# One product a head for the memory update, on the four column strips of TensorE

## The chip, the cores and the metric

The kernel runs on one core of one Trainium2 chip. The metric is the device time of one execution in microseconds (us). All five engines of the core are used: TensorE (PE, with PEld for its weight loads), VectorE (DVE), ScalarE (ACT), GpSimdE (POOL) and SyncE (SP), which only issues transfers.

## The reference

A layer normalisation feeds two branches whose results are added to the input: attention in four blocks of 512 tokens with a memory that is carried from block to block (16 heads of 28), and a gated feed-forward part.

```python
for s in range(N):                       # N = 4 blocks of L = 512 tokens
    qs, ks, vs = q[:, :, s], k[:, :, s], v[:, :, s]
    p = softmax(qs @ ks.T * scale + mask)
    a_dot = p @ vs
    pq = phi(qs)                         # phi(t) = t + 1 where t > 0, else exp(t)
    num = einsum("bhld,bhde->bhle", pq, M)
    den = einsum("bhld,bhd->bhl", pq, z)[..., None] + 1e-6
    outs.append(g * (num / den) + (1.0 - g) * a_dot)
    pk = phi(ks)
    M = M + einsum("bhld,bhle->bhde", pk, vs)
    z = z + einsum("bhld->bhd", pk)
return x + concat(outs) @ wo + (sigmoid(xn @ w_gate) * (xn @ w_up)) @ w_down
```

M is 28 x 28 a head, z a vector of 28. The kernel keeps z as one more column of M, by a column of ones beside the values.

## The kernel before

**Stages.** In a front part, the four blocks of tokens are normalised, turned, and projected to values (L361, pv), keys and queries (L381, pp); products in a split form of float32 take 11 passes each. The feed-forward part (L255, L181), the attention's scores (L639) and its sums over values (L725) follow, woven into each other by a hand-made plan, and the output projection (L824) ends the kernel. All of the change lies in the front part.

**A block of the front part** runs over `values` for four groups of 128 tokens, then `keys_queries` for seven groups of 128 columns (k = 0 to 6; four hold keys, which share the fourth with queries). Behind them, by `if`s on k, stand:

- `key_rows(k - 2)`: four transposes (pk, L401) bring a group of phi(keys) to token rows, and ScalarE copies them to kn (L403);
- `update(b, i)` (L405 to L416): the memory of four heads at a time, i = 0 to 3. Four products over 128 tokens each make a 112 x 128 tile (pmm) of phi(keys) of 4 heads by values of 4 heads. Only its diagonal blocks (28 x 32) are wanted, so VectorE multiplies it by `heads`, a mask of ones and zeros that GpSimdE builds (L522 to L527), and adds it to the memory of before. Updates 0 and 1 stand at k = 4 and 5, updates 2 and 3 at k = 6. Blocks 0, 1 and 2 update; block 3 does not;
- `turn`: transposes of the next block's tokens (pt, L103).

**The memory** is `mst[n][i]`, two sets of four tiles of 112 rows (28 a head) by 128 columns (32 a head).

**Reading the memory.** `keys_queries` stores phi(queries) to DRAM (fd, L394); `phi_queries` (L418) reads 112 rows of four heads back as phi; `recall` (L423) multiplies the memory by phi (n, L427), and VectorE divides the result. The recalls of blocks 1 and 2 are run between the values of the next block, those of block 3 between its projections.

**Order.** In the front part TensorE, ScalarE and VectorE run in the order in which the code is written (`tc.manual_schedule(engines=FRONT)`); GpSimdE and SyncE have an order that the framework sets. Accumulators have eight banks: pk, pmm and n share the tags "m" and "pd", of one bank each.

Of the kernel before, what the change touches and what calls it, by code (L numbers as in the profile page):

```python
# [9 lines left out]
F32 = mybir.dt.float32  # L10
F32R = mybir.dt.float32r
AF = mybir.ActivationFunctionType
ALU = mybir.AluOpType
# [3 lines left out]
P = 128  # L17
D = 448
H = 16
DH = 28  # L20
S = 2048
NB = 4
L = 512
NT = 4
F = 1792
NF = F // P
HG = 4
NG = H // HG
GW = HG * DH
# [40 lines left out]
def kernel(  # L70
# [10 lines left out]
    nc = tc.nc  # L81
    V, A, G, T = nc.vector, nc.scalar, nc.gpsimd, nc.tensor

    keep = ctx.enter_context(tc.tile_pool(name="keep", bufs=1))
    dram = ctx.enter_context(tc.tile_pool(name="dram", bufs=1, space=DRAM))
# [37 lines left out]
    def bank(name, tag):  # L123
        return ps.tile([P, L], F32, name=name, tag=tag, bufs=banks[tag])
# [5 lines left out]
    def pad(pool, nbytes):  # L130
        pool.tile([P, nbytes // 4], F32, name="pad", tag="pad", bufs=1)
# [3 lines left out]
    def weigh(pool, num, g, add):  # L135

        r = pool.tile([P, 16], F32, name="rc", bufs=2)
        n3 = num.rearrange("p (m c) -> p m c", c=32)
        if add:
            V.tensor_scalar_add(r, n3[:, :, DH], add)  # L140
            V.reciprocal(r, r)
        else:
            V.reciprocal(r, n3[:, :, DH])
        V.scalar_tensor_tensor(n3[:, :, :DH], n3[:, :, :DH], g, r.unsqueeze(2).to_broadcast([P, 16, DH]),
                               op0=ALU.mult, op1=ALU.mult)

    qd = [dram.tile([2 * D, 2, L], F32, name=f"qd{b}") for b in range(NB)]
    fd = [dram.tile([D, L], F32, name=f"fd{b}") for b in range(NB)]
    vd = [dram.tile([P, NT, H * 32], F32, name=f"vd{b}") for b in range(NB)]
    od = [dram.tile([H * 32, L], F32, name=f"od{b}") for b in range(NB)]  # L150

# [2 lines left out]
    def eight_k(dtype, name):  # L154
        return mid.tile([P, 8, 256], dtype, name=name, tag="8k")
# [144 lines left out]


    with tc.tile_pool(name="front", bufs=2) as sb, tc.manual_schedule(engines=FRONT):
        heads = sb.tile([P, P], F32, name="heads", bufs=1)
        pad(sb, 192)
        stage = eight_k(F32, "stage").rearrange("p (c a) n -> p c (a n)", c=4)
        vst = eight_k(F32, "vst").rearrange("p (t a) (h c) -> p t (a h) c", t=NT, c=32)
        wv = [late_pair("wv") for _ in range(4)]
        wv = [wv[c // 2][:, c % 2, :] for c in range(8)]
        wqk = [sb.tile([P, 8, P], F32R, name=f"wqk{c}", bufs=1) for c in range(7)]
        mst = [[sb.tile([GW, P], F32, name=f"mst{n}_{i}", bufs=1) for i in range(NG)] for n in range(2)]  # L310
        one = sb.tile([P, 1], F32, name="one", bufs=1)
        kn = eight_k(F32, "kn").rearrange("p (t a) n -> p t (a n)", t=NT)

# [55 lines left out]
        def values(b, t):  # L369
            pv = bank("pv", "p")  # L370
            value_terms(b, t, pv, EARLY[1] if b == 0 else TERMS)
            store_values(b, t, pv)
# [29 lines left out]
            n = min(P, D - c * P)  # L402
            A.activation(kn[:, :, c * P:c * P + n], pk.rearrange("p (t n) -> p t n", t=NT)[:, :, :n], AF.Copy)  # L403

        def update(b, i):  # L405

            pmm = bank("pmm", ("pd", "m")[i % 2])
            for t in range(NT):
                T.matmul(pmm[:GW, :P], kn[:, t, i * GW:(i + 1) * GW], vst[:, t, HG * i:HG * (i + 1), :],  # L409
                         start=t == 0, stop=t == NT - 1)  # L410
            if b == 0:
                V.tensor_mul(mst[1][i], pmm[:GW, :P], heads[:GW])
            else:
                dm = sb.tile([GW, P], F32, name="dm")
                V.tensor_mul(dm, pmm[:GW, :P], heads[:GW])
                V.tensor_add(mst[(b + 1) % 2][i], mst[b % 2][i], dm)  # L416

        def phi_queries(b, i):  # L418
            phi = sb.tile([GW, L], F32, name="phi", tag="e", bufs=5)
            nc.sync.dma_start(phi, fd[b][i * GW:(i + 1) * GW])  # L420
            return phi

        def recall(b, i, phi):  # L423
            ts = sb.tile([P, L], F32, name="ts", bufs=1)
            tb = sb.tile([P, L], F32, name="tb", bufs=2)
            n2 = bank("n2", ("m", "pd")[i % 2])
            T.matmul(n2, mst[b % 2][i], phi, start=True, stop=True)  # L427
            V.transpose(ts, n2)
            weigh(sb, ts, gate[:, i:i + 1], MEM_EPS)
            V.transpose(tb, ts)  # L430
            nc.gpsimd.dma_start(od[b][P * i:P * (i + 1)], tb)
# [28 lines left out]
        def split_qk(c):  # L460
            r = raw_qk[c].rearrange("p (c n) -> p c n", c=4)
            A.activation(wqk[c][:, 0:4, :], r, AF.Copy)
            G.tensor_sub(wqk[c][:, 4:8, :], r, wqk[c][:, 0:4, :].bitcast(F32))
# [18 lines left out]
        p3, xn, st, y = {}, {}, {}, {}  # L482
# [20 lines left out]
        for t in range(2):  # L503
# [15 lines left out]
        turn_low(3)  # L519
        split_qk(1)  # L520
        split_qk(2)
        G.memset(heads, 1.0)  # L522
        h3 = heads.rearrange("p (j c) -> p j c", c=32)
        G.affine_select(h3, h3, pattern=[[-DH, HG], [0, 32]], base=0, channel_multiplier=1,
                        compare_op=ALU.is_ge, fill=0.0)
        G.affine_select(h3, h3, pattern=[[DH, HG], [0, 32]], base=DH - 1, channel_multiplier=-1,
                        compare_op=ALU.is_ge, fill=0.0)  # L527

        ffn = gated()
        for b in range(NB):  # L530
            last = b == NB - 1
            phi, xn = {}, {}
            if b > 1:
                phi = {i: phi_queries(b - 1, i) for i in range(NG)}
            st = None
            for t in range(3 if b == 0 else 0, NT):
                values(b, t)
                if b > 1 and t > 0:
                    recall(b - 1, t - 1, phi[t - 1])
                if b == 0:  # L540
                    split_qk(t)
                if last:
                    continue
                if t == (3 if b == 0 else 0):
                    mv, vh = statistics(b + 1, 0, NT)
                if t == (3 if b == 0 else 0):
                    st = mv, vh, root(vh)
                if t == (3 if b == 0 else 2):
                    A.activation(one, ident[:, 0:1], AF.Exp)
            if st and b > 0:  # L550
                st = rstd(*st)
                for n in range(2):
                    xn[n] = normalise(b + 1, n, *st[n])
            e = {}
            for k, c in enumerate((3, 4, 5, 6, 0, 1, 2) if last else range(7)):
                e[c] = keys_queries(b, c)
                if b == 0 and c + 4 < 7:
                    split_qk(c + 4)
                if k == 0:
                    if b > 1:  # L560
                        recall(b - 1, NG - 1, phi[NG - 1])
                    if b == 0:
                        st = rstd(*st)
                    if b == 0:
                        A.activation(gate, gate, AF.Exp, scale=-1.0)
                        V.tensor_scalar_add(gate, gate, 1.0)
                        V.reciprocal(gate, gate)
                        V.tensor_scalar(gate_n, gate, -1.0, 1.0, op0=ALU.mult, op1=ALU.add)
                if (b, k) in ((0, 3), (1, 0)):
                    with tc.issue_after(stored[b, c]):  # L570
                        nc.sync.dma_start(acc[b + 2], x_block(b + 2))
                if (b, k) in ((2, 1), (3, 0)):
                    with tc.issue_after(stored[b, c]):
                        next(ffn)
                if last:
                    if k > 0:
                        next(ffn)
                    if 2 <= k < 6:
                        phi[k - 2] = phi_queries(b, k - 2)
                    if k > 4:  # L580
                        begin[k - 5]()
                        recall(b, k - 5, phi[k - 5])
                    continue
                if 2 <= k < 6:
                    key_rows(k - 2, e[k - 2])
                if 4 <= k:
                    update(b, k - 4)
                if k == 6:
                    update(b, 3)
                n = k - 1 if b == 0 else k + 1  # L590
                if 2 <= n < 6:
                    turn(b + 1, n - 2, xn[n - 2])
                if 0 <= n < 4 and n not in xn:
                    xn[n] = normalise(b + 1, n, *st[n])
                if b == 2 and k == 6:
                    next(ffn)
            if last:
                for i in range(2):
                    for _ in range(FILLS[i]):
                        next(ffn)  # L600
                    if i == 0:
                        begin[2]()
                    recall(b, i + 2, phi[i + 2])
# [3 lines left out]
    sb = ctx.enter_context(tc.tile_pool(name="att", bufs=1, reuse_waits="tile"))  # L607
# [234 lines left out]
    with tc.manual_schedule(engines=MANUAL):  # L842
        next(steps)
        k = sum(FILLS) + 6
# [46 lines left out]
```

## Time and profile before

| | |
|---|---|
| time, three runs | 685.53, 685.65, 686.12 us; median 685.65 |
| profiled execution, first to last instruction | 684.2 us (its device time is not shown apart from this span) |
| TensorE busy | 678.0 us, 99% |
| VectorE, ScalarE, GpSimdE busy | 570.1, 338.5, 141.6 us |
| front part | about 0 to 156 us |
| passes of the update (L409) | 96, from 34.4 to 115.0 us |
| VectorE's part of the update (L412, L415, L416) | 20 operations, 5.6 us |

A row of the profile's timeline has the start, the time from the first start to the last end, the engine, the line, the operation, what it writes and reads, the shapes, and how many instructions it joins; in brackets the idle time of the engine before it and what ended that. `128*112 128x128` for a product means 128 rows by 112 columns of weights, and a result of 128 columns a row from 128 columns of moving data. A row of a group has count, shortest, median and longest duration in ns, and the first and the last start; a row of the groups by shape ends with busy us and mean ns, then the idle time. `PEldq` marks what TensorE's sequencer does, a wait for a semaphore here. A row of the table by stretches has the stretch, its length, busy time and count of PE, PEld, DVE, ACT and POOL, the granted TensorE clock, the busy share of the transfer engines and GB/s.

### The profile page before, as it was taken

To read this page: it belongs to the slowest core of one execution; us is meant where nothing else is said; L and a number is where in the kernel's file an instruction comes from. 1 tells how busy PE (TensorE), PEld (TensorE's weight loads), DVE (VectorE), ACT (ScalarE), POOL (GpSimd) and SP (SyncE) were. 2 spreads that over 40 slices of the span, in tenths; PEclk is the share of its full clock that TensorE was granted. 3 is DMA by queue.
4 is the path that set the end of the run, shared out by engine and by line. 5 is a ranking of instruction groups with operands and counts; after the bars stand their busy time and mean duration, and the time that the engine had idled before them with its cause. 6 is when DMAs were issued, how large, how long until landed. Compare 5 with 4: busy or idle time off the path is not lost.

```text
span 684.2 us, 10501 instructions
## 1 busy us (share of the span) xinstructions
PE 678.0 (99%) x3594; PEld 566.7 (83%) x3594; DVE 570.1 (83%) x995; ACT 338.5 (49%) x563; POOL 141.6 (21%) x349
## 2 busy tenths in 40 slices
PE   8999999999999999999999999999999999999998
PEld 7898878778888888888888878788787887888897
DVE  6765696767799899999999899899998999899854
ACT  4836555343365445645456455455554555545320
POOL 3500010101212232232212213133121231221000
PEclk9999999999999999999999999999999999999999
DMA  8446656696223332252424343333353332523352
GB/s 268 173 159 224 214 195 256 234 336 194 71 67 97 104 90 68 57 150 54 108 57 101 91 110 69 100 57 99 84 94 94 97 69 68 115 63 92 86 165 104
DMA packets 45940, 84.37 MB, mean 123 GB/s; under 512 B 6336, under 2 KB 20544, under 8 KB 45376
## 3 DMA queue, kind: packets, MB, share of 16 engines
q1 hardware_dynamic: 42736, 76.26, 37.0%
q0 software_dynamic: 3008, 7.34, 5.2%
q8 instruction: 28, 0.46, 0.3%
q14 instruction: 24, 0.20, 0.1%
q10 hardware_dynamic: 144, 0.11, 0.0%
HBM read 51.05 MB, written 32.64 MB: 122 GB/s over the span
## 4 chain that ended last, share of the span: by engine, by line
PE 97%; DMA 1%; DVE 1%; SPq 0%; ACT 0%; issue 0%; DVEq 0%
PE pgu L255 41%; PE pd L181 20%; PE pp L381 10%; PE st L639 6%; PE pa L725 5%; PE po L824 5%; PE pv L361 5%; PE pmm L409 2%; PE n L427 2%; DMA acc<-in_x 1%; PE pt L103 1%; PE pk L401 1%; DVE stats L320 0%; DVE xs L110 0%; DVE xn L346 0%
## 5 line engine op out<-in xcount | busy, mean ns | idle before, releaser
L255 PE MATMUL pgu<-xs,wgu 128*128 128x512 f32 x1232 | 302.6, 393 | 0.0
L255 PEld LDWEIGHTS pgu<-xs,wgu 128*128 128x128 f32 x1232 | 228.9, 188 | 46.3 <-issue 2.0
L181 PE MATMUL pd<-wdn,hh 128*128 128x448 f32 x672 | 155.3, 366 | 0.0
L181 PEld LDWEIGHTS pd<-wdn,hh 128*128 128x128 f32 x672 | 122.7, 188 | 11.6 <-issue 0.8
L654 POOL TENSOR_SCALAR_AFFINE_SELECT w<-w 128x256 f32<-128x256 f32 (+1 forms) x160 | 76.0, 478 | 231.5 <-ACT w L643 162.4
L707 ACT ACTIVATE w<-w 128x1024 f32<-128x1024 f32 (+1 forms) x96 | 87.8, 915 | 57.6 <-DVE w L703 57.6
L643 ACT ACTIVATE w<-st 128x512 f32<-128x512 f32 x128 | 75.6, 592 | 61.4 <-PE st L639 58.5
L703 DVE TENSOR_TENSOR w<-w,mb 128x1024 f32<-128x1024 f32 (+1 forms) x96 | 100.5, 1054 | 0.8
L661 DVE TRANSPOSE_TENSOR_REDUCE mx<-w 128x32 f32<-128x1024 f32 x64 | 78.9, 1233 | 6.6 <-POOL w L654 6.5
L381 PE MATMUL pp<-xs,wqk 128*128 128x512 f32 x308 | 77.7, 401 | 0.0
L183 DVE TENSOR_TENSOR acc<-pd,acc 128x448 f32<-128x448 f32 x112 | 67.5, 602 | 5.6 <-PE pd L181 5.5
L278 ACT ACTIVATE hh<-sg 128x512 fp32r<-128x512 f32 x56 | 35.4, 631 | 67.9 <-DVE sg L272 46.0
L381 PEld LDWEIGHTS pp<-xs,wqk 128*128 128x128 f32 x308 | 56.8, 188 | 13.4 <-issue 2.4
L639 PE MATMUL st<-qk 84*128 84x128 f32 (+3 forms) x256 | 62.0, 313 | 0.0
L262 ACT ACTIVATE sg<-pgu 128x512 f32<-128x512 f32 x56 | 33.2, 592 | 50.8 <-PE pgu L255 48.9
L639 PEld LDWEIGHTS st<-qk 84*128 84x128 f32 x256 | 47.9, 189 | 8.7 <-issue 1.4
L272 DVE SCALAR_TENSOR_TENSOR sg<-sg,pgu 128x512 f32<-128x512 f32 x56 | 37.7, 673 | 11.2 <-PE pgu L255 11.2
L388 DVE TENSOR_TENSOR qk<-pp,qk 128x512 fp32r<-128x512 f32 x28 | 19.3, 688 | 29.8 <-ACT e L386 23.7
L689 DVE STREAM_TRANSPOSE mb<-top 128x1024 f32<-128x1024 f32 x32 | 39.5, 1235 | 3.3 <-POOL top L686 3.2
L361 PE MATMUL pv<-wv,xs 128*128 128x448 f32 x176 | 39.6, 376 | 0.4 <-DVE xs L110 0.3
L281 DVE SCALAR_TENSOR_TENSOR hh<-sg,hh 128x512 fp32r<-128x512 f32 x56 | 38.1, 680 | 0.9 <-ACT hh L278 0.9
L725 PE MATMUL pa<-w,vv 128*32 128x128 f32 (+3 forms) x512 | 37.8, 436 | 0.0
(100 smaller groups left out, 636.0 us busy)
## 6 DMA issues: line engine op xcount, KB each, us to landing
qk<-qd SPq DMA_DIRECT2D x192, 112.0 KB
qd<-qk SPq DMA_DIRECT2D x28, 512.0 KB
raw<-in_w_ffn SPq DMA_DIRECT2D x14, 512.0 KB
vd<-vst SPq DMA_DIRECT2D x4, 1024.0 KB
vv<-vd SPq DMA_DIRECT2D x16, 256.0 KB
od<-w POOLq DMA_DIRECT2D x16, 256.0 KB, 4.2
sums<-od SPq DMA_DIRECT2D x32, 128.0 KB
out<-acc SPq DMA_DIRECT2D x15, 224.0 KB
```

What stands on the lines that cost most here:

```text
L181: T.matmul(pd[:, :D], l, r, start=n == 0, stop=n == len(mms) - 1)
L183: V.tensor_add(acc[b][:, t, :], pd[:, :D], acc[b][:, t, :])
L255: T.matmul(dst, wgu[f][:, w, side * P:(side + 1) * P], xs[b][:, a, :], start=n == 0, stop=n == len(TERMS) - 1)
L361: T.matmul(pv[:, :D], xs[b][:, a, t * P:(t + 1) * P], wv[w], start=n == 0, stop=n == len(TERMS) - 1)
L381: T.matmul(pp, wqk[c][:, w, :], xs[b][:, a, :], start=n == 0, stop=n == len(TERMS) - 1)
L639: T.matmul(st[:, at:at + L - kb * P], self.qk[:KS, 1, h, kb * P:(kb + 1) * P], self.qk[:KS, 0, h, kb * P:], start=True, stop=True)
L643: A.activation(w, st, AF.Copy)
L654: G.affine_select(d, d, pattern=pattern, base=0, channel_multiplier=-1, compare_op=ALU.is_ge, fill=MASK)
L661: V.tensor_reduce(self.mx[:, 32 * h:32 * h + 32], w3[:, h, :2 * L].rearrange("p (b n) -> p b n", n=32), axis=mybir.AxisListType.X, op=ALU. ...
L703: V.tensor_sub(w, w, m)
L707: A.activation(w, w, AF.Exp, scale=SCALE)
L725: T.matmul(pa[32 * j:32 * j + 32, kb * P:], self.vv[:, kb, 32 * j:32 * j + 32], self.pairs[j // 2].block(j % 2, kb), start=kb == 0, stop=k ...
```

## The change

An update of a block is one call at k = 6 behind the last projection. Each of the 16 heads has its own products: 28 columns of phi(keys) as weights, the head's 32 columns of values as moving data, four groups of tokens. Head j of a group of four goes to rows 32 j of the accumulator, and so to column strip j; the group i to columns 32 i. All 16 heads end in one bank, 28 of 32 rows a strip. The memory is one tile a set, 128 rows (32 a head) by four groups of 128 columns, cleared once at the start, so that what lies off the diagonal and in the four spare rows stays zero; VectorE copies or adds the four strips' rows to the diagonal blocks. phi is read back as 32 rows a head: four rows of the next head, which meet zero rows of the memory. The last head's four rows lie behind the 448 rows of fd, and are filled with zeros by three stores of GpSimdE at the start. The mask `heads` is gone.

```diff
-    fd = [dram.tile([D, L], F32, name=f"fd{b}") for b in range(NB)]
+    fd = [dram.tile([D + 4, L], F32, name=f"fd{b}") for b in range(NB)]
...
-        heads = sb.tile([P, P], F32, name="heads", bufs=1)
...
-        mst = [[sb.tile([GW, P], F32, name=f"mst{n}_{i}", bufs=1) for i in range(NG)] for n in range(2)]
+        mst = [sb.tile([P, NG, HG, 32], F32, name=f"mst{n}", bufs=1) for n in range(2)]
...
-        def update(b, i):
-
-            pmm = bank("pmm", ("pd", "m")[i % 2])
-            for t in range(NT):
-                T.matmul(pmm[:GW, :P], kn[:, t, i * GW:(i + 1) * GW], vst[:, t, HG * i:HG * (i + 1), :],
-                         start=t == 0, stop=t == NT - 1)
-            if b == 0:
-                V.tensor_mul(mst[1][i], pmm[:GW, :P], heads[:GW])
-            else:
-                dm = sb.tile([GW, P], F32, name="dm")
-                V.tensor_mul(dm, pmm[:GW, :P], heads[:GW])
-                V.tensor_add(mst[(b + 1) % 2][i], mst[b % 2][i], dm)
+        def update(b):
+
+            pmm = bank("pmm", "m")
+            for i in range(NG):
+                for t in range(NT):
+                    for j in range(HG):
+                        h = HG * i + j
+                        T.matmul(pmm[32 * j:32 * j + DH, 32 * i:32 * i + 32], kn[:, t, DH * h:DH * (h + 1)],
+                                 vst[:, t, h, :], start=t == 0, stop=t == NT - 1)
+            p3 = pmm[:, :P].rearrange("p (i c) -> p i c", c=32)
+            for j in range(HG):
+                strip = slice(32 * j, 32 * j + DH)
+                new, old = (mst[(b + n) % 2][strip, :, j, :] for n in (1, 0))
+                if b == 0:
+                    V.tensor_copy(new, p3[strip])
+                else:
+                    V.tensor_add(new, p3[strip], old)
 
         def phi_queries(b, i):
-            phi = sb.tile([GW, L], F32, name="phi", tag="e", bufs=5)
-            nc.sync.dma_start(phi, fd[b][i * GW:(i + 1) * GW])
+
+            phi = sb.tile([P, L], F32, name="phi", tag="e", bufs=5)
+            rows = fd[b][i * GW:(i + 1) * GW + 4]
+            nc.sync.dma_start(phi, bass.AP(rows.tensor, rows.offset, [[DH * L, HG], [L, 32], [1, L]]))
             return phi
...
-            T.matmul(n2, mst[b % 2][i], phi, start=True, stop=True)
+            T.matmul(n2, mst[b % 2][:, i].rearrange("p j c -> p (j c)"), phi, start=True, stop=True)
...
-        G.memset(heads, 1.0)
-        h3 = heads.rearrange("p (j c) -> p j c", c=32)
-        G.affine_select(h3, h3, pattern=[[-DH, HG], [0, 32]], base=0, channel_multiplier=1,
-                        compare_op=ALU.is_ge, fill=0.0)
-        G.affine_select(h3, h3, pattern=[[DH, HG], [0, 32]], base=DH - 1, channel_multiplier=-1,
-                        compare_op=ALU.is_ge, fill=0.0)
+        for n in range(2):
+            G.memset(mst[n], 0.0)
+        for b in range(1, NB):
+            nc.gpsimd.dma_start(fd[b][D:].rearrange("a (c n) -> (a c) n", n=P), mst[1][:16, 0].rearrange("p j c -> p (j c)"))
...
-                if 4 <= k:
-                    update(b, k - 4)
                 if k == 6:
-                    update(b, 3)
+                    update(b)
```

TensorE's order before, in block 1, from the fifth projection of keys and queries (k = 4) on; pp are projections, pk transposes of keys, pmm updates, pt transposes of the next block, pv its values, n recalls, with the size of the result and the count of products:

```order
L381 MATMUL pp<-xs_66,wqk_119 128x512 x11
L401 MATMUL pk<-ident,e 128x128 x4
L409 MATMUL pmm<-vst,kn 112x128 x4
L103 MATMUL pt<-ident,xn 128x128 x4
L381 MATMUL pp<-xs_66,wqk_120 128x512 x11
L401 MATMUL pk<-ident,e 128x128 x4
L409 MATMUL pmm<-vst,kn 112x128 x4
L381 MATMUL pp<-xs_66,wqk_121 128x512 x11
L409 MATMUL pmm<-vst,kn 112x128 x8
L361 MATMUL pv<-wv,xs_67 128x448 x22
L427 MATMUL n_953<-phi,mst_0_126 128x512
```

And the same place in the changed kernel:

```order
L380 MATMUL pp<-xs_66,wqk_118 128x512 x11
L400 MATMUL pk<-ident,e 128x128 x4
L103 MATMUL pt<-ident,xn 128x128 x4
L380 MATMUL pp<-xs_66,wqk_119 128x512 x11
L400 MATMUL pk<-ident,e 128x128 x4
L380 MATMUL pp<-xs_66,wqk_120 128x512 x11
L411 MATMUL pmm<-vst,kn 28x32 x64
L360 MATMUL pv<-wv,xs_67 128x448 x22
L433 MATMUL n_1030<-phi,mst_122 128x512
```

The two updates between the projections have gone to the others behind the last projection, and 16 products have become 64 smaller ones.

GpSimdE's order before, at the start of the kernel; ident is the identity of the transposes, vst the values, wv the value weights:

```order
masks.py:197 MEMSET ident 128x128
L522 MEMSET heads 128x128
masks.py:199 ISA
masks.py:199 AFFINE_SELECT ident<-ident 128x128
L453 MEMSET vst 128x64x4
L524 AFFINE_SELECT heads<-heads 128x128
L526 AFFINE_SELECT heads<-heads 128x128
L458 TENSOR_TENSOR wv<-wv_raw,wv 128x448 x4
```

And in the changed kernel:

```order
masks.py:197 MEMSET ident 128x128
L529 MEMSET mst_121 128x512
masks.py:199 ISA
masks.py:199 AFFINE_SELECT ident<-ident 128x128
L459 MEMSET vst 128x64x4
L529 MEMSET mst_122 128x512
L531 DMA fd_84<-mst_122 16x128
L531 DMA fd_85<-mst_122 16x128
L531 DMA fd_86<-mst_122 16x128
L464 TENSOR_TENSOR wv<-wv_raw,wv 128x448 x4
```

The clears of the memory stand in the places of the mask, one of them ahead of the identity's mask, and three stores of zeros have been added.

## The prediction

> **What bounds the kernel now.** I read the page first: its busy shares, the clock row, and the chain that ended last.
>
> ```profile
> span 684.2 us, 10501 instructions
> PE 678.0 (99%) x3594; PEld 566.7 (83%) x3594; DVE 570.1 (83%) x995; ACT 338.5 (49%) x563; POOL 141.6 (21%) x349
> PEclk9999999999999999999999999999999999999999
> PE 97%; DMA 1%; DVE 1%; SPq 0%; ACT 0%; issue 0%; DVEq 0%
> PE pgu L255 41%; PE pd L181 20%; PE pp L381 10%; PE st L639 6%; PE pa L725 5%; PE po L824 5%; PE pv L361 5%; PE pmm L409 2%; PE n L427 2%; DMA acc<-in_x 1%; PE pt L103 1%; PE pk L401 1%; DVE stats L320 0%; DVE xs L110 0%; DVE xn L346 0%
> ```
>
> TensorE works without a break at the full granted clock, and 97% of the chain is its own products. So almost any time that the change adds to or takes from TensorE's stream moves the end by as much. The updates (pmm, L409) stand in the chain; VectorE's and GpSimdE's share of the change does not, unless it makes TensorE wait.
>
> **What the update costs now.** The timeline of block 0, where two updates stand alone, and the group over all blocks:
>
> ```profile
> 34.42 1.04 PE L409 MATMUL pmm<-vst,kn 128*112 128x128 f32 x8
> 35.29 0.60 PE L103 MATMUL pt<-ident,xn 128*128 128x128 f32 x4
> 38.71 1.04 PE L409 MATMUL pmm<-vst,kn 128*112 128x128 f32 x8
> 39.58 0.60 PE L103 MATMUL pt<-ident,xn 128*128 128x128 f32 x4
> L409 PE MATMUL pmm<-vst,kn x96: 271/273/273, 34.4 to 115.0; 128*112 128x128 f32 x96
> ```
>
> A product in float32 is two passes in the trace, each with its weight load: 4 groups of 4 tokens are 16 products, 32 passes a block, 96 in three blocks. Eight passes take 35.29 - 34.42 = 0.87 us, 109 ns each. (The 273 ns is one pass from end to end; passes overlap.) So an update of one block costs 32 x 0.109 = 3.49 us of TensorE, and all of them 10.5 us, 1.5% of the span.
>
> **What the new update costs.** 64 products a block, each 28 columns of weights by 32 columns of values: 128 passes, 128 weight loads. No row shows such a pass. The nearest is the attention's sum over values (pa, L725), which already puts four heads side by side on the four column strips; its first unit:
>
> ```profile
> 203.22 0.16 PEld L725 LDWEIGHTS pa<-w,vv 128*32 128x32 f32 x8
> 203.68 0.13 PEld L725 LDWEIGHTS pa<-w,vv 128*32 128x32 f32 x4 [0.30 <-issue]
> 204.11 0.13 PEld L725 LDWEIGHTS pa<-w,vv 128*32 128x32 f32 x4 [0.30 <-issue]
> 204.43 0.13 PEld L725 LDWEIGHTS pa<-w,vv 128*32 128x32 f32 x4 [0.19 <-issue]
> 205.52 0.90 PEld L181 LDWEIGHTS pd<-wdn,hh 128*128 128x128 f32 x5 [0.20 <-issue]
> 203.23 2.36 PE L725 MATMUL pa<-w,vv 128*32 128x512 f32 x32
> 205.52 1.48 PE L181 MATMUL pd<-wdn,hh 128*128 128x448 f32 x6
> ```
>
> Weight loads come in fours, one a strip, so the strips do run together. Between the fours lie 204.11 - 203.68 = 0.43 us for 512 moving columns and 0.32 us for 384: 0.84 ns a column. Two prices follow.
>
> *The array.* 32 columns are 27 ns for four passes at once. 128 passes are 32 fours, 32 x 27 = 0.86 us. This is the least that the update can take.
>
> *The feed.* The array takes four passes in 27 ns only if eight instructions (four loads, four products) reach it in that time. How fast TensorE's sequencer brings them is seen from its semaphore waits, which it executes in order while the products before them are still queued. I take the first wait of a score (L639) behind the 32 passes of a pa unit:
>
> ```profile
> 261.53 2.36 PE L725 MATMUL pa<-w,vv 128*32 128x512 f32 x32
> L639 PEldq EVENT_SEMAPHORE  x1: 51/51/51, 262.4 to 262.4; - x1
> 290.18 0.64 PE L725 MATMUL pa<-w,vv 128*32 128x512 f32 x4
> L639 PEldq EVENT_SEMAPHORE  x1: 51/51/51, 291.1 to 291.1; - x1
> L639 PEldq EVENT_SEMAPHORE  x1: 51/51/51, 204.3 to 204.3; - x1
> 347.33 2.36 PE L725 MATMUL pa<-w,vv 128*32 128x512 f32 x32
> L639 PEldq EVENT_SEMAPHORE  x1: 51/51/51, 348.4 to 348.4; - x1
> ```
>
> In the units at 261.53 and 290.18 the score follows at once, and its wait stands 0.87 and 0.92 us after the unit's start. In those at 203.23 and 347.33 six pd passes lie between, and it stands 1.07 and 1.07 us after. So six pairs of load and product took the sequencer about 0.18 us longer: 30 ns a pair. The rows give tenths, so it may be 0.10 to 0.22 us, 17 to 37 ns a pair. In those 0.18 us no four leaves (one at 204.11, the next at 204.43), so I read the wait as the sequencer's own pace and not as a full queue. 30 ns is more than the array's 27 / 4 = 7 ns a pass. **The feed, not the array, sets the new update's length**, and it is my value because it is the one measured pace of this resource.
>
> Some passes are already queued when the update's turn comes. That is read where the sequencer has reached a pa unit's wait while the unit starts later:
>
> ```profile
> L725 PEldq EVENT_SEMAPHORE  x1: 51/51/51, 199.8 to 199.8; - x1
> 199.81 0.39 PEld L181 LDWEIGHTS pd<-wdn,hh 128*128 128x128 f32 x2
> 200.21 2.43 PEld L255 LDWEIGHTS pgu<-xs,wgu 128*128 128x128 f32 x11
> 202.68 0.42 PEld L639 LDWEIGHTS st<-qk 84*128 84x128 f32 x2
> ```
>
> 2 + 11 + 2 = 15 loads run before the unit's: the sequencer is some 16 pairs ahead. So 128 - 16 = 112 pairs at 30 ns: 3.36 us a block.
>
> *Into the strips and out.* The pa unit takes 205.52 - 203.23 = 2.29 us; its columns, 2 x (512 + 384 + 256 + 128) x 0.84 ns, are 2.15 us: 0.14 us more. Behind it the load of pd waits 0.20 us, where loads elsewhere lie beside products. So 0.14 to 0.34 us a switch; I take 0.3, since the idle 0.20 us is on TensorE's path. The old updates have no such gap.
>
> A block's update: 3.36 + 0.3 = 3.66 us against 3.49, **+0.17 us; three blocks +0.5 us**. Ends: at 17 ns 1.90 + 0.14, -1.45 a block, -4.3 in all; at 37 ns 4.14 + 0.34, +0.99 a block, +3.0 in all.
>
> [...]
>
> **The other edits, by what hides them.**
>
> ```profile
> 74.44 0.36 ACT L403 ACTIVATE kn<-pk 128x256 f32<-128x256 f32 x1
> 77.73 0.60 PE L409 MATMUL pmm<-vst,kn 128*112 128x128 f32 x4
> 78.09 4.66 PE L361 MATMUL pv<-wv,xs 128*128 128x448 f32 x22
> 82.58 0.59 PE L427 MATMUL n<-phi,mst 112*128 112x512 f32 x1
> 79.53 3.27 SPq L420 DMA_DIRECT2D phi<-fd  x3
> L415 DVE TENSOR_TENSOR dm<-pmm,heads 112x128 f32<-112x128 f32 x8 | 2.2, 280 | 0.0
> L416 DVE TENSOR_TENSOR mst<-mst,dm 112x128 f32<-112x128 f32 x8 | 2.3, 292 | 0.3
> ```
>
> - *Waits of the update.* It needs the keys' last copy (kn, done at 74.80), which its second half needed before; 16 passes earlier in the stream go (1.75 us), so it would start about 74.7 where it now starts at 76.4, and the copy comes some 0.9 us earlier with its transposes. Its last quarter alone needs that copy. No wait; if there were one, values (pv) of the next block stand behind it.
> - *VectorE.* Eight operations of 0.28 to 0.29 us a block become four: 1.15 us instead of 2.29. The recall's product (n) at 82.58 needs them; between lie 22 pv passes, 4.5 us. Nothing gained, nothing lost.
> - *Reads of phi.* 128 rows of 2 KB instead of 112, a seventh more. The issues end by 82.80 and the last two are used after 22 more passes. The extra wait on the zero rows is for a transfer of the first microseconds. Zero; if that cover went, TensorE would wait at n.
> - *Recall's product* has 128 rows instead of 112; time goes by columns. Zero.
> - *The beginning.* GpSimdE clears two tiles of 512 columns, not one of 128, and issues three stores of 8 KB:
>
> ```profile
> 0.95 0.20 POOL L522 MEMSET heads<- 128x128 f32 x1
> 1.42 0.31 POOL L453 MEMSET vst<- 128x256 f32 x1
> 8.61 2.27 POOL L458 TENSOR_TENSOR wv<-wv_raw,wv 128x448 fp32r<-128x448 f32 x2 [6.24 <-ACT wv L457]
> 2.67 7.49 DMA acc<-in_x
> 8.00:12.00 4.00, 3.06 (x15) 2.22 (x16) 2.96 (x8) 2.78 (x7) 3.40 (x4) 1.00 1.02 388
> ```
>
> The first clear is put ahead of the identity's mask, so the warm-up products start some 0.3 us later (about 0.1 us per 128 columns). GpSimdE is then idle 6.24 us before it is needed, which holds the clears and three issues. The chain there is the load of x, landing at 10.16, with the transfer engines full (share 1.02, 388 GB/s): 24 KB more are 0.06 us. I take **+0.1 us**, 0 to 0.5.
>
> **Sum.** +0.5 + 0.1 = +0.6 us on a span of 684.2. The runs shown have a median of 685.65, 1.45 us above that span for what lies around it; the same difference gives **686.3 us**.
>
> **The rivals.**
>
> - *The array sets the pace* (the change does what it says). 0.86 + 0.3 = 1.16 us a block, -2.33; three blocks -7.0, with the beginning 678.8. For it: eight loads of pa run within 0.16 us when they are already queued. Against it: only 16 of 128 pairs are queued. It decides in full from a feed of 7 ns a pass; all that is under 17 ns is counted here. Chance 0.10.
> - *The granted clock falls* (slower). At 30 ns a pair a four takes 120 ns of which the array works 27; for 3.4 us TensorE is mostly idle inside. The clock row shows 1.00 through the stretch from 8 to 12, where TensorE was busy 3.06 of 4.00 us, so gaps of that size are borne; an update is thinner. At half clock the 4.5 us of pv behind each update would last up to 4.5 us more while it holds; half of it, 2.2 us, in three blocks is +6.7: 693. It decides if the row of the clock leaves 1.00 near 45, 78 or 115 us. Chance 0.06. [...]
> - *The feed is slower still* for float32 passes than for those six, 50 ns: 112 x 0.05 + 0.3 - 3.49 = +2.4 a block, 693. Against it: old updates ran at 109 ns a pair, which only says less than that. Chance 0.04.
>
> **How the numbers follow.** The forecast (feed of 17 to 37 ns) has 0.80. A measurement here tells about 0.2%, 1.37 us, from no change. Within the forecast, 0.17 of it lies more than that below (a feed under 24 ns) and 0.23 more than that above (over 32 ns). Faster: 0.10 + 0.80 x 0.17 = 0.24; slower: 0.06 + 0.04 + 0.80 x 0.23 = 0.28; same 0.48. The range takes in the ends of the feed and of the switch with the beginning, -4.3 to +3.0 + 0.5: 681.4 to 689.2. What it leaves out is the three rivals, 0.20.
>
> **What would show it.** The new passes near 41, 75 and 112 us: starts 25 to 35 ns apart behind a first burst, an update 3.4 to 3.9 us from its first load to the next pv or pt. Passes in fours every 27 ns, or 1.2 us for an update, would prove the first rival. A gap of 0.2 us in the loads before pv confirms the switch. VectorE's four operations should end before n, and no n should wait for phi. Wrong in kind would be a wait of TensorE on GpSimdE's or DMA's work, or a granted clock below 1.00.

## The result, and the profile after

The changed kernel takes 693.38 us (median of four runs, 691.55 to 695.04) against 685.61 us (four runs beside it). Its ratio to the kernel before is 1.0112, with an interval from 1.0094 to 1.0129: slower by 7.8 us. The forecast was 686.3 us, and its range ended at 689.2. The profiled execution took 691.55 us, with a span of 689.8 where it was 684.2.

The page of the changed kernel, its busy shares, clock and chain:

```profile
span 689.8 us, 11085 instructions
PE 674.2 (98%) x3882; PEld 559.8 (81%) x3882; DVE 568.9 (82%) x987; ACT 338.3 (49%) x563; POOL 143.5 (21%) x351
PEclk9999999999999999999999999999999999999999
PE 92%; DMA 5%; DVE 1%; SPq 0%; issue 0%; ACT 0%; DVEq 0%
PE pgu L255 40%; PE pd L181 20%; PE pp L380 10%; PE st L641 6%; PE pa L727 5%; PE po L826 5%; DMA phi<-fd 4%; PE pv L360 3%; DMA acc<-in_x 1%; PE n L433 1%; PE pt L103 1%; PE pk L400 1%; PE pmm L411 0%; ACT qk L381 0%; DVE stats L319 0%
```

Two entries of the chain have changed. The updates (pmm) have gone from 2% to 0%: they became much cheaper, which the prediction gave a chance of 0.10. And the read of phi, which was not in the chain at all, now has 4% of it. TensorE's busy time fell by 3.8 us (678.0 to 674.2) while the span grew by 5.6. So TensorE now stands still for about 9 us more. The groups of the recall's product n show where; first the kernel before, with no idle time behind the second bar, then the changed kernel:

```profile
L427 PE MATMUL n<-phi,mst 112*128 112x512 f32 x24 | 12.3, 591 | 0.0
L433 PE MATMUL n<-phi,mst 128*128 128x512 f32 x24 | 13.0, 623 | 9.7 <-DMA phi<-fd 8.7 <-DVE vh L321 0.9
```

The timeline has the single waits. First block 1, from the update on, then the recalls of block 3:

```profile
72.36 1.44 PE L411 MATMUL pmm<-vst,kn 128*28 128x32 f32 x128
73.72 4.68 PE L360 MATMUL pv<-wv,xs 128*128 128x448 f32 x22
79.28 1.10 PE L433 MATMUL n<-phi,mst 128*128 128x512 f32 x2 [0.88 <-DVE vh L321]
79.82 2.78 PE L360 MATMUL pv<-wv,xs 128*128 128x448 f32 x11
83.69 1.12 PE L433 MATMUL n<-phi,mst 128*128 128x512 f32 x2 [1.10 <-DMA phi<-fd]
...
150.85 1.13 PE L433 MATMUL n<-phi,mst 128*128 128x512 f32 x2 [0.63 <-DMA phi<-fd]
155.64 1.10 PE L433 MATMUL n<-phi,mst 128*128 128x512 f32 x2 [1.82 <-DMA phi<-fd]
161.39 1.10 PE L433 MATMUL n<-phi,mst 128*128 128x512 f32 x2 [3.05 <-DMA phi<-fd]
```

The 22 passes of pv stand behind the update at 73.72, 1.36 us after its start; in block 0 the update took 1.21 us. The first n comes 3.30 us earlier than before (79.28 against 82.58), so the updates did save time; then one n after the other waits. In block 3 the last n is at 161.39, and from there to the end every product is 5.5 to 5.6 us later than before.

Adding up the starts of such products against the kernel before: after block 1's update pv is 4.4 us ahead, and at the end of its recalls 1.5. Block 2's update brings this to 3.4 and its recalls take it to 0.8. Block 3's recalls turn that into 5.5 behind. The recalls lose about 11.7 us, and the updates win 6.

The granted clock stayed at 1.00 in this execution. The other three (693.25, 693.52 and 695.04 us) have mean clocks of 0.997, 0.998 and 0.995, so a part of the median's 7.8 us is a lower clock; the section on the prediction comes back to it.

### The profile page after: what moved, and what is told of

It reads as the page before. It is cut to its first block, busy times and chain, and to the rows that moved or that the text cites. A ratio compares the mean times of both kernels' runs of the same rounds, so it can differ in the third digit from the quotient of the medians.

```text
span 689.8 us, 11085 instructions
## 1 busy us (share of the span) xinstructions
PE 674.2 (98%) x3882; PEld 559.8 (81%) x3882; DVE 568.9 (82%) x987; ACT 338.3 (49%) x563; POOL 143.5 (21%) x351
## 4 chain that ended last, share of the span: by engine, by line
PE 92%; DMA 5%; DVE 1%; SPq 0%; issue 0%; ACT 0%; DVEq 0%
PE pgu L255 40%; PE pd L181 20%; PE pp L380 10%; PE st L641 6%; PE pa L727 5%; PE po L826 5%; DMA phi<-fd 4%; PE pv L360 3%; DMA acc<-in_x 1%; PE n L433 1%; PE pt L103 1%; PE pk L400 1%; PE pmm L411 0%; ACT qk L381 0%; DVE stats L319 0%
```

## The experiments

**Theory A**: phi is now read by one transfer (DMA) of 4 strips of 32 rows, and only 4 of the 16 transfer engines carry it; it lands late, and TensorE waits at n. **Rival B**: the larger count of rows, or the zero rows, make it late. **Rival C**: the shorter updates alone make the recalls come too early for it. All comparisons are with 685.78 us for the kernel before in the first four experiments, and 685.75 in the last two.

What speaks for A before any run is the share of the transfer engines in a stretch with reads of phi in flight. That share, ahead of the GB/s at the end of a row, is a mean over the 16 transfer engines. The kernel before:

```profile
83.50:84.50 1.00, 1.00 (x7) 0.93 (x6) 0.82 (x2) 0.46 (x2) 0.00 (x0) 1.00 0.99 354
```

The changed kernel:

```profile
80.50:83.00 2.50, 2.09 (x11) 1.62 (x9) 2.36 (x5) 0.37 (x1) 0.00 (x0) 1.00 0.27 102
```

0.99 of 16 engines is 15.8, 0.27 is 4.3. The outermost step of the read was 112 rows and is 4 strips now; that its count sets the number of engines is, at this point, the author's reading of these two rows.

### heads4: the read cut into four, one per head

```diff
-            nc.sync.dma_start(phi, bass.AP(rows.tensor, rows.offset, [[DH * L, HG], [L, 32], [1, L]]))
+            for j in range(HG):
+                nc.sync.dma_start(phi[32 * j:32 * j + 32], rows[DH * j:DH * j + 32])
```

> The changed kernel with each read of phi cut into four, one per head: 32 rows that lie one after the other, in place of one read of 4 x 32 rows. Same rows, same bytes. Theory A (the read as 4 x 32 rows is carried by 4 of the 16 transfer engines, lands late, and TensorE waits for it at the recalls' product n): the quarter reads use all 16, no n waits for phi, and what is left is the gain of the updates, 3 x 2.1 to 2.3 us and 0.3 us of the beginning: 678.5 to 680.0 us. Rival B (a seventh more rows, or the zero rows, make the read late): n still waits, 690 us or more. Rival C (recalls come too early because the updates are shorter, whatever the read looks like): waits of about half, 684 to 688. All: 12 loads become 48, 36 issues more on SyncE.

Measured: 683.33 us (683.09 to 683.94), ratio 0.9966, interval 0.9954 to 0.9978. Between the medians lie 10.05 us, with rows, bytes and zero rows unchanged, so B falls. Between the profiled executions, whose clocks are 1.000 and 0.999, it is 8.5 us (691.55 - 683.09); the rest fits the lower clock of the changed kernel's other runs. One thing differs besides the read: in heads4, and in the two kernels built on it, the last n of block 3 stands 18 passes of the feed-forward part behind the one ahead of it, where it was 7, though the lines that place it are the same. The cut did not need this: the packets of the last group's reads (the pieces of a transfer, in the trace's records) end at 148.5, and in the old place that n would have come at about 152.2 (an estimate, 149.69 and the 2.47 us from 153.46 to 155.93 in the kernel before). 683.33 is outside what A expected, and just under C's 684 to 688: two waits at n remain. The group of n in heads4 has them with their releasers behind the second bar:

```profile
L434 PE MATMUL n<-phi,mst 128*128 128x512 f32 x24 | 12.4, 597 | 2.0 <-DVE vh L321 1.2 <-DMA phi<-fd 0.9
```

And its timeline:

```profile
79.61 1.10 PE L434 MATMUL n<-phi,mst 128*128 128x512 f32 x2 [1.18 <-DVE vh L321]
115.62 1.10 PE L434 MATMUL n<-phi,mst 128*128 128x512 f32 x2 [0.86 <-DMA phi<-fd]
```

Both are the first n of a block. SyncE's queue in heads4 shows why: of the first group's four reads one is issued before the last store of features (fd<-e at 75.13), three behind it, and an issue takes 0.46 us (6.95 for 15). `SPq` marks the issues on that queue.

```profile
72.60 0.53 SPq L427 DMA_DIRECT2D phi<-fd  x1
74.47 0.33 SPq L388 DMA_DIRECT2D qd<-qk  x1
75.13 1.34 SPq L393 DMA_DIRECT2D fd<-e  x1
76.53 6.95 SPq L427 DMA_DIRECT2D phi<-fd  x15
```

So a part of C is true as well: these waits are there because n now comes about 3 us earlier.

### old_update_4x28: the old updates with the new shape of read

```diff
-            nc.sync.dma_start(phi, fd[b][i * GW:(i + 1) * GW])
+            rows = fd[b][i * GW:(i + 1) * GW]
+            nc.sync.dma_start(phi, bass.AP(rows.tensor, rows.offset, [[(DH - 1) * L, HG], [L, DH], [1, L]]))
```

> The kernel before, with its old updates, but phi read as 4 x 28 rows (strips 27 rows apart, so that they cannot be taken as one run of 112 rows; the recall then reads other rows, of the same count and bytes). Theory A: the read runs on 4 transfer engines, n waits for phi, 692 to 698 us (the changed kernel lost some 12 us at n; here the longer updates cover a part of each wait). Rivals B (rows and zero rows) and C (shorter updates): nothing changes, 685.0 to 686.3 us.

Measured: 692.5 us (692.04 to 692.92), ratio 1.0097, interval 1.0083 to 1.011, at the near end of A's expectation. The bytes are those of before. A window of this kernel with its reads in flight has 4 engines' share again:

```profile
81.50:84.00 2.50, 2.50 (x12) 1.91 (x11) 2.04 (x6) 1.21 (x3) 0.00 (x0) 1.00 0.26 93
```

And in its timeline TensorE waits for phi in block 3 alone:

```profile
155.19 1.10 PE L428 MATMUL n<-phi,mst 112*128 112x512 f32 x2 [1.39 <-DMA phi<-fd]
160.67 1.10 PE L428 MATMUL n<-phi,mst 112*128 112x512 f32 x2 [2.77 <-DMA phi<-fd]
```

The shape of the read costs 6.7 us without the new updates. Only 4.2 us of this are the two waits. Behind the second one TensorE ran at half clock for a while, which costs some 1.7 us more (an estimate: the clock records of the trace have 0.5 for 3.41 us from 162.13 on, half of which is lost). A window shows it, with the granted clock of 0.71 as its mean:

```profile
160.00:165.00 5.00, 4.33 (x11) 3.15 (x12) 3.15 (x7) 1.06 (x2) 0.00 (x0) 0.71 0.45 145
```

In blocks 1 and 2 the old updates, 2.3 us longer each, still hide it; the short ones don't. That is why the changed kernel's recalls lost more than this, and C's part again.

### two_of_64: two reads of 2 strips each

```diff
-            nc.sync.dma_start(phi, bass.AP(rows.tensor, rows.offset, [[DH * L, HG], [L, 32], [1, L]]))
+            for j in range(0, HG, 2):
+                nc.sync.dma_start(phi[32 * j:32 * j + 64],
+                                  bass.AP(rows.tensor, rows.offset + j * DH * L, [[DH * L, 2], [L, 32], [1, L]]))
```

> The changed kernel with each read of phi cut into two of 2 x 32 rows. Theory A, in the form that the count of the outermost step says how many transfer engines carry the read: two engines, and the same two for both halves; a block's four loads take some 20 us instead of 10, and the time is 705 to 730 us. If it is only the size of one read or its three levels that make it slow: at most as slow as the changed kernel, 685 to 694 us.

Measured: 726.1 us (one run). Twice the reads, half the size, and much slower. A window of this kernel in which TensorE stood still:

```profile
82.00:84.00 2.00, 0.00 (x0) 0.00 (x0) 0.00 (x0) 0.00 (x0) 0.00 (x0) 0.60 0.13 51
```

And its timeline behind it:

```profile
84.44 2.05 PE L435 MATMUL n<-phi,mst 128*128 128x512 f32 x2 [5.78 <-DMA phi<-fd]
85.50 4.51 PE L360 MATMUL pv<-wv,xs 128*128 128x448 f32 x11
```

0.13 of 16 engines is 2.1, and 51 GB/s half of the 102 with an outermost step of 4. Several reads in flight did not make it four engines, so they ran on the same two. Among the shapes run here the share goes with the count of the outermost step: 0.99 with 112 rows, 0.27 and 0.26 with 4 strips, 0.13 with 2, and 1.04 with 32 rows (heads4_early, below). Not all of the 726.1 us is waiting: TensorE waited 30.6 us for phi at n, and the mean granted clock of the run is 0.976.

### strip_after_strip: the same products, one strip at a time

```diff
-            for i in range(NG):
-                for t in range(NT):
-                    for j in range(HG):
+            for j in range(HG):
+                for i in range(NG):
+                    for t in range(NT):
                         h = HG * i + j
```

> As heads4, but the update's loop over the four strips is outermost: the same 64 products and the same strips, 16 in a row on each strip, so that neighbours never lie on different strips but for three switches. If strips working side by side are what made the update short, a pass now takes 32 columns at 0.84 ns, 27 ns: 128 x 27 = 3.5 us a block instead of 1.2, three blocks +6.7 us on heads4, 685 to 687 us. If the sequencer's feed alone sets the 8 to 9 ns a pass: as heads4 within 0.7 us.

Measured: 687.68 us (687.08 to 688.33), ratio 1.0026, interval 1.0016 to 1.0037; 4.35 us above heads4, a little over the expected end. The groups of pmm show the updates' busy time on TensorE in us, first behind the bar. The kernel before:

```profile
L409 PE MATMUL pmm<-vst,kn 128*112 128x128 f32 x96 | 11.9, 272 | 0.0
```

heads4:

```profile
L411 PE MATMUL pmm<-vst,kn 128*28 128x32 f32 x384 | 3.9, 197 | 0.0
```

strip_after_strip:

```profile
L411 PE MATMUL pmm<-vst,kn 128*28 128x32 f32 x384 | 10.9, 194 | 0.0
```

Its timeline in block 1:

```profile
74.72 3.64 PE L411 MATMUL pmm<-vst,kn 128*28 128x32 f32 x128
78.30 4.68 PE L360 MATMUL pv<-wv,xs 128*128 128x448 f32 x22
```

The starts of the single passes, in ns from one to the next, from the records of the last two kernels (block 1; the first passes, then some from the middle):

```
heads4             7 7 6 30 6 7 7 9 6 7 7 9 7 6 7 9 ...  4 12 5 12 4 13 5 11 5 13 ...
strip_after_strip  49 30 29 29 29 29 29 30 29 29 29 ...  29 30 29 29 29 29 29 30 29 ...
```

On one strip a pass comes every 29 ns, 0.91 ns a column. With four strips in turn four come in 30 ns for the first 32 passes, and in 34 ns (8.5 a pass) later on. The gain of the new updates is therefore the strips' working side by side (whether the 29 ns of one strip are the columns alone or also the load of the weights is not separated), and the same 128 passes without it take 3.58 us (78.30 - 74.72), as much as the old update's 3.49. There is no wait at n in this kernel: with the long update the quarter reads are in time. That is 2.0 of the 2.75 us by which its distance to heads4, 4.35 us, falls short of 3 x 2.37 = 7.1 (3.58 - 1.21 a block). The two profiled executions, 688.33 and 683.09, are 5.2 us apart, as 7.1 - 2.0 = 5.1 would have it.

### heads4_early: the first two groups' reads issued one step earlier

```diff
-                phi = {i: phi_queries(b - 1, i) for i in range(NG)}
+                phi = {**ahead, **{i: phi_queries(b - 1, i) for i in range(2, NG)}}
...
+                if b > 0 and k == 5:
+                    ahead = {i: phi_queries(b, i) for i in range(2)}
```

> heads4 with the reads of the first two groups issued one step earlier, ahead of the keys of the last piece of features, instead of behind the last store of features. Theory: in heads4 the first recall waited 1.2 us in block 1 and 0.9 us in block 2 because three of its four quarter reads stood on SyncE behind that store; put ahead of it they land before n, and TensorE gains these 2.1 us: 680.5 to 682.0 us. Rival: the wait was for VectorE (the profile names vh of the statistics as its releaser), which this leaves as it is: 683.0 to 684.0 us.

Measured: 680.94 us (680.66 to 681.36), ratio 0.9929, interval 0.9915 to 0.9942. **This version beats both kernels.** No n waits any more, on a span of 679.1 us, and what was said to be released by VectorE (vh) is gone with VectorE's work unchanged: this n starts at 79.03, before vh does at 79.16. The releaser of that row was wrong, it was the read. The group of n in this kernel, with no idle time behind the second bar:

```profile
L434 PE MATMUL n<-phi,mst 128*128 128x512 f32 x24 | 12.2, 591 | 0.0
```

SyncE's queue in block 1, with the first two groups' reads ahead of the last store of features (six of the eight here; two went out at 69.05):

```profile
72.48 4.14 SPq L427 DMA_DIRECT2D phi<-fd  x6
76.71 0.38 SPq L388 DMA_DIRECT2D qd<-qk  x1
77.14 0.42 SPq L393 DMA_DIRECT2D fd<-e  x1
77.61 4.79 SPq L427 DMA_DIRECT2D phi<-fd  x8
```

With reads of 32 rows in flight the transfer engines are full, as they were with 112 rows:

```profile
79.00:80.50 1.50, 1.50 (x7) 0.97 (x7) 0.70 (x3) 0.64 (x2) 0.00 (x0) 1.00 1.04 276
```

### changed_early: the earlier issue without the cut

The edit is that of heads4_early, on the changed kernel with its reads of 4 strips.

> The changed kernel, its reads of 4 x 32 rows as they are, with only the reads of the first two groups issued one step earlier. Theory (the reads are slow because 4 engines carry them, so an earlier issue hides part of it): the waits of blocks 1 and 2, which cost 2.9 and 2.6 us there, shrink to 0 to 2 us each, and those of block 3 (6.2 us) stay: 686.5 to 690.5 us. Rival (the issue's place alone was at fault): all but block 3's go and block 3's too, 680 to 683 us.

Measured: 701.96 us (700.62 to 703.99), ratio 1.0238, interval 1.0222 to 1.0253. Both expectations missed: it lost another 8.6 us. In the profiled executions (702.12 against 691.55) the idle time before n grew by 4.1 us, 13.8 against 9.7. The rest fits the clock: it was granted at half for 13.65 us in three places (the clock records of the trace, mean 0.990), an estimated 6.8 us lost, behind waits of 3.4 to 4.3 us. The first two n of block 1 are indeed in time, but the third pays more, as its timeline shows:

```profile
79.31 1.02 PE L433 MATMUL n<-phi,mst 128*128 128x512 f32 x2
82.37 1.02 PE L433 MATMUL n<-phi,mst 128*128 128x512 f32 x2
89.30 1.64 PE L433 MATMUL n<-phi,mst 128*128 128x512 f32 x2 [3.70 <-DMA phi<-fd]
```

What held this read up stands in SyncE's queue in the same stretch:

```profile
72.64 3.14 SPq L426 DMA_DIRECT2D phi<-fd  x2
75.87 0.42 SPq L388 DMA_DIRECT2D qd<-qk  x1
76.35 0.58 SPq L393 DMA_DIRECT2D fd<-e  x1
83.66 1.11 SPq L426 DMA_DIRECT2D phi<-fd  x2
```

And in SyncE's waits there (us in total, how many, the longest):

```profile
SPq L426 <- DMA fd<-e: 8.6, 2, 6.6
```

The last store of features goes out at 76.35. The reads of the third and fourth group wait for it on SyncE and go out only from 83.66 on, 7.3 us later (the last row: 8.6 us in two waits, the longer 6.6). In heads4_early the store goes out at 77.14, and those waits add up to 1.1 us. Such a store seems to be carried by all engines (in heads4_early up to 50 of its packets of 4 KB start in half a microsecond, an estimated 410 GB/s, four times the 102 of four engines), so a share of it lies on the engines that still carry the reads of phi. That it queues behind them there fits the packets: those of 2 and 4 KB start at 58 to 86 in half a microsecond from 77 to 79 us, and at 4 to 24 from then until they end; the 102 GB/s of four engines are 25 of 2 KB. No run took the store to other engines, so this link is read from the trace and not shown by an experiment. The changed kernel has the same wait, with a store issued at 74.96 and reads that go out from 81.0 on.

## Why the prediction was wrong, point by point

- **"Reads of phi. … Zero"** is the step that failed. It counted rows and bytes ("a seventh more") and took the speed of the read from before. The bytes were not what changed: the outermost step of the access pattern went from 112 rows to 4 strips, and the reads ran at 102 GB/s on a quarter of the engines where they had 354. The prediction saw the place ("if that cover went, TensorE would wait at n") but gave it neither a price nor a chance, though the diff shows the new pattern. A wait of TensorE on a transfer, its own sign of being wrong in kind, is what came. The cost is the difference between the changed kernel and heads4_early, 693.38 - 680.94 = 12.4 us: 10.05 for the shape of the read (heads4; 8.5 where the clock stayed up), 2.4 for the place of its issue, which matters now that n comes earlier. That the forecast missed by only 7.1 us is luck: the next error has the other sign.
- **"The feed, not the array, sets the new update's length"**, 30 ns a pair, failed too, in the other direction. In heads4 the sequencer brought a load and its product at least every 8.5 ns, over the last 96 passes of an update. The 0.18 us between the score's waits were not its pace; the prediction read them so because no four left the array in that time. The first rival, with a chance of 0.10, was the true mechanism: it gave 1.16 us for an update and -2.33 a block, measured are 1.21 us and -2.28 (1.21 - 3.49). It also named its own proof, fours every 27 ns or 1.2 us for an update. That 1.16 is so near is in part chance: a four took 30 to 34 ns and not 27, and the switch less than the 0.3 us it counted.
- **The switch into the strips**, 0.3 us a block, was too long, and it stands at the other end. From the last load of an update to the next kind of load lie 0.04 us, not a gap of 0.2 us. Ahead of the update the loads do wait 0.36 us, but products fill most of it: from the start of the 11 passes of pp before it to the update it is 2.72 us (37.90 to 40.62), where it was 2.61 (39.94 to 42.55), so 0.1 us a block:

```profile
40.62 1.17 PEld L411 LDWEIGHTS pmm<-vst,kn 128*28 128x28 f32 x128 [0.36 <-issue]
...
41.50 0.29 PEld L411 LDWEIGHTS pmm<-vst,kn 128*28 128x28 f32 x22
41.83 0.42 PEld L103 LDWEIGHTS pt<-ident,xn 128*128 128x128 f32 x4
```

- **The granted clock at the updates**: 1.00 through them, as forecast. That rival did not come at the updates. (The prediction's trace has a window as thin as it feared, at its end: TensorE busy 0.79 of 4.20 us from 680.0 on, granted clock 1.00.) But a clock below 1.00, another of its signs, came elsewhere: the four runs of the changed kernel (691.55, 693.25, 693.52, 695.04 us) have mean clocks of 1.00, 0.997, 0.998 and 0.995. Only the first has a trace here, so where the others lost it stays open. Their distances from it, 1.7, 2.0 and 3.5 us, are what one, one and two stretches of 3.41 us at half clock would cost, 1.7 us each (an estimate from the stretch in old_update_4x28).
- **VectorE**: four operations a block, 1.18 us together, in place of eight, as forecast, and no n waited for them. **The beginning**: +0.1 us was forecast. The first projection starts 0.15 to 0.4 us earlier in each of these profiles, that of old_update_4x28 too, whose beginning is that of before. So the edits there cost nothing that can be seen.
- **The sum.** Rival one's 678.8 us would have been near the kernel without the slow reads: heads4_early has 680.94. Of the 2.1 us between, 0.7 are the updates: TensorE's stream gained 2.1 us in each of the three blocks (starts before and behind the updates, heads4_early against the kernel before), not 2.33. Another 0.63 are a new wait in its block 1, of pv for ScalarE's copy of the values:

```profile
76.72 2.47 PE L360 MATMUL pv<-wv,xs 128*128 128x448 f32 x11 [0.63 <-ACT vst L364]
```

The rest was not followed up.

## What to carry to other kernels

When a change gives a DMA another access pattern, count the engines that it will run on before its bytes: look at the outermost step (here reads of 112 and of 32 rows kept all 16 busy, 4 strips about 4, 2 strips 2), and price the read at the rate that such a shape was measured at (354, 102 and 51 GB/s for 112 rows, 4 and 2 strips) against the wait that it must beat. A step that becomes shorter takes cover away from every transfer behind it, so list those with the time each has left. Four passes of small products on four column strips in turn came in 30 to 34 ns here, where one strip alone took 29 ns for each, so an update made of many took a third of the time of the same products one strip after another (1.21 against 3.58 us). And a wait of TensorE may cost more than its length: here the clock was granted at half behind waits from 2.77 us (old_update_4x28) to 5.78 us (two_of_64), though not behind one of 3.05 us (the changed kernel), so look at the granted clock behind it.

## What the runs showed of the hardware

- One slow read can hold up others: with reads on 4 engines, what waited for a store issued behind them came 7.3 us after it (changed_early). Issuing the reads earlier made the kernel slower by 8.6 us, by longer waits and the lower clock behind them. That the store queues behind the reads is read from the trace, as said above.
- Reads of outermost step 2 in flight together used two engines, not four (share 0.13).
- A wait of TensorE cost twice in two_of_64. After 5.78 us without work, two passes of n took 2.05 us instead of 1.02, and eleven of pv 4.51 instead of 2.77. The window there has a granted clock of 0.50:

```profile
84.00:87.00 3.00, 2.56 (x4) 1.50 (x5) 0.47 (x1) 0.00 (x0) 0.00 (x0) 0.50 0.13 51
```

The length of the wait alone does not decide. Behind 3.05 us in the changed kernel the clock did not fall (n 1.10, and 1.00 granted from 160 to 165 us), behind 3.70 us in changed_early it did (n 1.64), and so it did in old_update_4x28, 1.5 us after a wait of only 2.77 us. The changed kernel:

```profile
160.00:165.00 5.00, 3.61 (x14) 2.71 (x15) 2.14 (x5) 1.06 (x2) 0.00 (x0) 1.00 0.41 151
```

Inside the kernel the stretches of half clock last 3.41 or 6.83 us in the clock records of these traces (3.41 in old_update_4x28; 13.65 in three places in changed_early). What decides beside the length of a wait was not shown: no run moved one of these waits alone.

- The profile's releaser can name the wrong engine where a wait has several sources: the 1.2 us of n "for vh" went when a read was issued earlier, and n then started before vh.
